# A two-layer long-convolution and FFN kernel: the plan's gaps refitted, and a new order for all engines

## The chip, the cores and the metric

The kernel runs on one core of a Trainium2 chip. The metric is the device time of one execution in microseconds (us). All data is bf16, all matmuls accumulate in f32 in PSUM.

Five engines work beside each other, each with a queue of its own: TensorE (PE in the profile, its weight loads are PEld), VectorE (DVE), ScalarE (ACT), GpSimd (POOL) and SyncE (SP, which in this kernel only issues DMAs).

## The reference

S = 2048 rows, D = 512 columns, F = 1792; x starts as `q`, and two equal layers follow, each a long convolution with gating and then a gated FFN:

```python
def _A_ref(q, k, v, shift_k, ssm_k, ssm_D):     # q is layernorm(x)
    k_shift = sum over t of k_pad[:, t:t + S, :] * shift_k[:, ks - 1 - t]     # 4 taps
    kv = k_shift * v
    ...
    y_f = kv_f * kf_f[None, :, :, :]            # FFTs of length 2*S of kv and ssm_k
    y = irfft(y_f)[:S].astype(bfloat16)
    y = y + kv * ssm_D
    return q * y

def _B_ref(x, w_gate, w_up, w_down):            # x is layernorm(x)
    return (silu(x @ w_gate) * (x @ w_up)) @ w_down

x = A_q
x = x + _A_ref(_layernorm(x), A_k, A_v, ...);  x = x + _B_ref(_layernorm(x), ...)
x = x + _A_ref(_layernorm(x), A_k, A_v, ...);  x = x + _B_ref(_layernorm(x), ...)
```

The convolution's result y does not depend on x and is the same in both layers, so it is computed once.

## The kernel before

**Tiles.** The 2048 rows are cut into 4 chunks c of 512 rows (128 partitions times 4 rows r). The convolution works chunk by chunk as products of discrete spectra, which are matmuls: the tables `fwd` and `inv` hold cosines and sines. For a chunk, `shift_mul` applies the 4 taps as matmuls with the diagonal matrices `dg`, `half` and `direct` bring the filter (`hs`) and the input (`vt`) to spectra (buffers `ev`/H, G and X in the profile, all by `evacuate`, L431), DVE multiplies and adds spectra, and `inverse_half` or `inverse` turn them back into `Yk`. The FFN works on units (layer, c, h) of 256 rows, h = 0 or 1: `gate_up` has 112 pairs of PSUM banks `pf` (the pair is one gate product, which ACT turns by Silu into `sg` on L974, and one up product, which ACT copies to `ht` on L977), DVE multiplies the two, and `down` accumulates in `pd`. PSUM has 4 banks of `pf`, 2 of `pc`, 2 of `pd`.

**Start.** The first chunk is what all else waits for: load `kn` (k's rows) and `hn` (the filter), transpose both on PE (`pt`, L378 and L489), taps (`ps<-dg,kTb`), spectra of filter and input, products, inverse (`m<-Z` on DVE L803, then PE `ps<-m,inv`, L809). Then `prologue(0, 0, 0, on_pe=True)` makes x + n*y, where n is the normalised x (ACT, L874), normalises again into `z`, transposes it on PE (`ptz`, L935) and copies it out as `zT`: row 0 on ACT (L940), the other on DVE. The first gate/up matmul (`pf<-zT,wg_sb`) needs both. For row 0 of the chunk, `prologue` does not wait for y to be in SBUF: DVE multiplies n by the PSUM bank itself (L918, `n<-n,ps`), and the ACT copy of the same bank to `Yk` (L729) is issued behind it by `evacuate_y(c, (0,))`. Every layer norm ends with a power -1/2 on POOL, `rstd<-ve,nhalf` (L826 for statistics of DVE, L855 for those of ACT, whose sums and squares are the `jk` rows of L840 and its neighbour); then `nmr` (L863, L867) and the normalising n or z.

**Later work.** From the first FFN unit on, the units' matmuls alternate with the convolution work of the next chunks. The last unit ends with one group of 512 columns (row 0) and the other row in parts of 320 and 192 columns (`TAIL`), each with its own copy or add and its own DMA (L1039 to L1055).

**Order.** Nothing is left to a scheduler. The program records 1,556 operations in a `Plan`, each with an engine, a cost in us, and the buffers it reads and writes; `Plan.add` derives the dependences (readers of one buffer don't depend on each other). The table `ORDER` gives each operation its place, and `Plan.order` goes through them in that order, sums the costs to a planned start and end for each, with a gap between an operation and one that needs its data (`SAME` on one engine, `CROSS` across engines, by the engine that produces), and gives each buffer the slot of its ring that comes free first by that plan. `Plan.issue` emits the operations in that order. So the order of each engine's queue is that of the table, and the planned times set only the ring slots and the dummy matmuls:

```python
                if start < warm_until and start - t > 0.5:
                    ...
                            n = int((start - t - (0.3 if t > 8.0 else 0.5 if t > 0.0 else 0.1)) / 0.106)
                            if n > 0:
                                warm(ring, i, n)
```

`warm` (L1307) writes 128-column products of ones into a free bank, in planned PE gaps of over 0.5 us before 32 us. `PW`, `PWA` and the 0.85 that `prologue` passes are the planned costs of the POOL power.

Of the kernel before, what the change touches and what calls it, by code (L numbers as in the profile page):

```python
# [9 lines left out]
P = 128  # L10
# [3 lines left out]
ACT = mybir.ActivationFunctionType  # L14
# [9 lines left out]
PW = 1.2  # L24
# [19 lines left out]
PWA = 2.4  # L44
# [9 lines left out]
SHARE = {(1, 0, 1): 2, (0, 2, 0): 2, (1, 3, 0): 2}  # L54
ORDER = [
# [1285 lines left out]
```

## Time and profile before

| | us |
|---|---|
| median of 3 runs | 343.18 (342.79 to 343.26) |
| span of the profiled execution | 341.1 |
| median less span | 2.1 |
| PE busy | 336.9 (99%), 2563 instructions |
| DVE busy | 282.4 (83%), 478 |
| ACT busy | 252.5 (74%), 496 |
| POOL busy | 37.3 (11%), 46 |
| last PE work ends at | 338.13 |

The span runs from the first to the last event of one profiled execution; the profiled execution has no other time of its own on record, so sums from the trace are made against its span, and the 2.1 us between span and median lie around it.  Busy times are shares of it; matmuls are pipelined, so a busy PE may still wait inside. A row of a time line has start and length in us, the engine, the line of the kernel, the operation, and output and input; a row of a group has the count, then the summed busy time and the mean in ns.

### The profile page before, as it was taken

The page shows a single profiled execution, that of the slowest core. Times are in us where ns is not written, and L with a number is a line of the kernel's source. Part 1 is how long each engine was busy: PE and PEld are TensorE (multiplying, and loading weights), DVE is VectorE, ACT ScalarE, POOL GpSimd, SP SyncE. Part 2 cuts the span into 40 slices and gives each one's busy share as a digit, 9 for nine tenths or more (in the row PEclk, how much of TensorE's full clock was granted, in tenths as well). Part 3 has the DMA queues.
Part 4 walks back from the last instruction along what each step waited for, and adds up shares of the span by engine and source line. Part 5 has one row for each costly group of instructions (what it writes and reads, how often), then busy time and mean ns, then how long its engine had stood idle before and what let it go on. Part 6 is the DMA issues. An engine that isn't in the chain of part 4 may idle for free.

```text
span 341.1 us, 6468 instructions
## 1 busy us (share of the span) xinstructions
PE 336.9 (99%) x2563; PEld 242.8 (71%) x2563; DVE 282.4 (83%) x478; ACT 252.5 (74%) x496; POOL 37.3 (11%) x46
## 2 busy tenths in 40 slices
PE   8999999999999999999999999999999999999996
PEld 7657858678687567768587756768685877777683
DVE  8899999999999999999999999889997533726022
ACT  7899999999977475778999973768665545545451
POOL 4000100002106100103100100101101000001000
PEclk9999999999999999999999999999999999999999
DMA  7999314050224175010110224010101110001111
GB/s 280 333 320 341 52 31 63 0 156 1 34 46 94 31 102 164 3 30 2 33 20 13 48 46 125 0 33 1 33 0 44 36 33 0 17 16 21 27 33 31
DMA packets 42088, 22.95 MB, mean 67 GB/s; under 512 B 33989, under 2 KB 39882, under 8 KB 42058
## 3 DMA queue, kind: packets, MB, share of 16 engines
q1 hardware_dynamic: 41904, 22.49, 26.0%
q8 instruction: 20, 0.33, 0.4%
q14 instruction: 10, 0.08, 0.1%
q10 hardware_dynamic: 154, 0.05, 0.1%
HBM read 12.33 MB, written 2.10 MB: 42 GB/s over the span
## 4 chain that ended last, share of the span: by engine, by line
PE 94%; ACT 3%; DMA 1%; SPq 0%; issue 0%; ACTq 0%
PE pf L323 57%; PE pd L994 28%; PE ps L323 6%; PE ps L470 2%; DMA kn<-in_A_k_dram 1%; ACT H L431 1%; ACT Yk L729 1%; ACT ks L526 0%; ACT n L874 0%; PE pt L378 0%; PE pt L489 0%; ACT zT L940 0%; ACT X L431 0%; SPq L354 0%; ACT xc L1052 0%
## 5 line engine op out<-in xcount | busy, mean ns | idle before, releaser
L323 PE MATMUL pf<-zT,wg_sb 128*128 128x256 bf16 (+1 forms) x872 | 110.3, 276 | 0.0
L323 PE MATMUL pf<-zT,wu_sb 128*128 128x256 bf16 (+1 forms) x872 | 110.0, 275 | 0.1
L994 PE MATMUL pd<-wd_sb,ht 128*128 128x512 bf16 (+1 forms) x462 | 106.2, 373 | 0.0
L323 PEld LDWEIGHTS <-wu_sb 128*128 128x128 bf16 x872 | 85.3, 98 | 18.9 <-issue 0.6
L323 PEld LDWEIGHTS <-wg_sb 128*128 128x128 bf16 x872 | 85.3, 98 | 17.3
L977 ACT CAST ht<-pf 128x512 bf16<-128x512 f32 x112 | 65.0, 592 | 23.0 <-PE pf L323 22.8
L974 ACT ACTIVATE sg<-pf 128x512 bf16<-128x512 f32 x112 | 66.6, 606 | 20.8 <-PE pf L323 17.3
L994 PEld LDWEIGHTS <-ht 128*128 128x128 bf16 x462 | 45.0, 98 | 44.1
L979 DVE TENSOR_TENSOR ht<-ht,sg 128x1024 bf16<-128x1024 bf16 (+1 forms) x61 | 38.9, 642 | 19.8 <-ACT ht L977 13.7
L826 POOL TENSOR_TENSOR rstd<-ve,nhalf 128x2 f32<-128x2 f32 x24 | 25.1, 1047 | 192.6 <-DVE ve L824 192.6
L821 DVE BATCH_NORM_STATS2 bnst<-xc 128x6 f32<-128x512 bf16 x48 | 31.8, 684 | 0.5
L1075 ACT CAST dn<-pd 128x512 bf16<-128x512 f32 x30 | 17.2, 590 | 17.5 <-PE pd L994 17.5
L431 ACT ACTIVATE X<-ps 128x512 bf16<-128x512 f32 x32 | 18.9, 606 | 10.5 <-PE ps L323 10.0
L1078 DVE TENSOR_TENSOR xc<-xc,dn 128x1024 bf16<-128x1024 bf16 x15 | 10.3, 687 | 16.8 <-ACT dn L1075 16.8
L669 DVE TENSOR_TENSOR t<-X,G 128x2048 bf16<-128x2048 bf16 x18 | 21.9, 1218 | 0.1
L665 DVE TENSOR_TENSOR t<-X,G 128x2048 bf16<-128x2048 bf16 x18 | 21.9, 1219 | 0.0
L855 POOL TENSOR_TENSOR rstd<-ve,nhalf 128x2 f32<-128x2 f32 x8 | 8.4, 1052 | 78.5 <-ACT ve L853 78.5
L679 DVE TENSOR_TENSOR Z<-Z,t 128x2048 bf16<-128x2048 bf16 x12 | 14.7, 1221 | 0.3
L677 DVE TENSOR_TENSOR t<-t,t 128x2048 bf16<-128x2048 bf16 x12 | 14.6, 1220 | 0.2
L431 ACT ACTIVATE H<-ps 128x512 bf16<-128x512 f32 x24 | 14.2, 612 | 0.0
L901 DVE TENSOR_TENSOR n<-n,Yk 128x1024 bf16<-128x1024 bf16 x15 | 10.3, 690 | 3.1 <-ACT n L874 1.9
L323 PE MATMUL ps<-hs,fwd 128*128 128x512 bf16 x40 | 12.7, 379 | 0.1
(103 smaller groups left out, 321.8 us busy)
## 6 DMA issues: line engine op xcount, KB each, us to landing
hn<-in_A_ssm_k_dram SPq DMA_DIRECT2D x4, 512.0 KB, 5.5
vt<-in_A_v_dram SPq DMA_DIRECT2D x4, 512.0 KB, 5.6
xc<-in_A_q_dram SPq DMA_DIRECT2D x4, 512.0 KB, 4.9
out_dram<-xc SPq DMA_DIRECT2D x15, 128.0 KB, 1.8
wg_sb<-in_B_w_gate_dram SPq DMA_DIRECT2D x1, 1792.0 KB
wu_sb<-in_B_w_up_dram SPq DMA_DIRECT2D x1, 1792.0 KB, 8.0
wd_sb<-in_B_w_down_dram SPq DMA_DIRECT2D x1, 1280.0 KB, 11.6
kn<-in_A_k_dram SPq DMA_DIRECT2D x1, 512.0 KB, 4.3
```

The source lines that it names most:

```text
L323: nc.tensor.matmul(o, lhsT=lhsT, rhs=rhs, start=(n == 0), stop=(n == len(terms) - 1))
L431: add("ACT", act(D), lambda: nc.scalar.activation(out=view(), in_=ps.t[:], func=ACT.Copy, scale=scale), r=[ps], w=[(buf, keys)], conv=conv)
L665: dve(n * D, lambda t1=t1, part=part: nc.vector.tensor_mul(out=t1.t[:], in0=x.t[:, sl, 0, :], in1=g.t[:, sl, part, :]), [(x, key(slots, (0 ...
L669: dve(n * D, lambda t2=t2, part=part: nc.vector.tensor_mul(out=t2.t[:], in0=x.t[:, sl, 1, :], in1=g.t[:, sl, 1 - part, :]), [(x, key(slots ...
L679: dve(n * D, lambda t1=t1, part=part: nc.vector.tensor_add(out=z.t[:, sl, part, :], in0=z.t[:, sl, part, :], in1=t1.t[:]), [t1], [zk], con ...
L821: add("DVE", 0.6, lambda st=st, i=i: nc.vector.bn_stats(out=st.t[:], in_=xs[c].t[:, i, :]), r=[(xs[c], (i,))], w=[st])
L826: add("POOL", pw, lambda: nc.gpsimd.tensor_tensor(out=rstd.t[:], in0=ve.t[:], in1=nhalf.t[:].to_broadcast((P, n)), op=ALU.pow), r=[ve, nha ...
L974: add("ACT", act(D), lambda ps=ps, sl=sl: nc.scalar.activation(out=sg.t[:, sl], in_=ps.t[:], func=ACT.Silu), r=[ps], w=[(sg, (b,))], due=( ...
L977: add("ACT", act(D), lambda ps=ps, sl=sl: nc.scalar.copy(out=ht.t[:, sl], in_=ps.t[:]), r=[ps], w=[(ht, (b,))], due=(us[0], at, 1.5, "a"))
L979: dve(n * m * W, lambda: nc.vector.tensor_mul(out=ht.t[:], in0=ht.t[:], in1=sg.t[:]), [sg], [ht], due=(us[0], (k + n) / NF, 0.0, "h"))
L994: nc.tensor.matmul((pds[o] if not cs.start else pds[HP]).t[:, cs], lhsT=ht.t[:, q, at, o * P:(o + 1) * P], rhs=wt["d"].t[:, ft, cs], start ...
L1075: add("ACT", act(D), lambda o=o: nc.scalar.copy(out=dn.t[:, o, :], in_=pds[o].t[:]), r=[pds[o]], w=[(dn, (o,))], due=(unit, 1.0, 3.0, "h"))
```

## The change

It has three parts. The matmuls are the same ones, and so is the arithmetic.

1. The plan's gaps and three of its costs are other numbers: `SAME` for ACT 0.12 for 0.05; `CROSS` for PE 0.2 for 0.3, DVE 0.14 for 0.2, ACT 0.15 for 0.25, POOL 0.05 for 0.15; the POOL power 0.69 everywhere.
2. `ORDER` is a new table of the same 1,556 operations, so each engine's queue has a new order; ring slots and dummy matmuls follow from it (35 dummies for 32).
3. Copies go through a helper, `copy_out`, which can hold the same copy for ACT and for DVE; the set `FLIP` that would swap them is empty, so every copy stays on its engine. Its forms are `activation(Copy)` on ACT, where some lines had `nc.scalar.copy`, and `tensor_scalar` times 1.0 on DVE, where some had `tensor_copy`.

```diff
-PW = 1.2
+PW = 0.69
...
-PWA = 2.4
+PWA = 0.69
...
+FLIP = set()
 ORDER = [
-    0, 5, 1, 2, 3, 21, 16, 6, 14, 8, 15, 66, 69, 10, 7, 9, 4, 11, 34, 12, 17, 18, 13, 19, 20, 35, 26, 120, 121, 131, 27, 30, 31, 39, 37, 40, 36, 41,
+    6, 37, 2, 5, 1, 8, 19, 0, 3, 4, 28, 40, 61, 7, 10, 9, 11, 12, 26, 20, 22, 21, 16, 23, 25, 46, 54, 65, 78, 107, 18, 42, 17, 38, 15, 33, 14, 30,
...
-    SAME = {"PE": 0.0, "DVE": 0.12, "ACT": 0.05, "POOL": 0.1, "SP": 0.0}
-    CROSS = {"PE": 0.3, "DVE": 0.2, "ACT": 0.25, "POOL": 0.15, "SP": 0.0}
+    SAME = {"PE": 0.0, "DVE": 0.12, "ACT": 0.12, "POOL": 0.1, "SP": 0.0}
+    CROSS = {"PE": 0.2, "DVE": 0.14, "ACT": 0.15, "POOL": 0.05, "SP": 0.0}
...
-    def add(self, eng, cost, emit, r=(), w=(), lat=None, due=None, conv=False, slack=0.0, after=(), dest=None):
+    def add(self, eng, cost, emit, r=(), w=(), lat=None, due=None, conv=False, slack=0.0, after=(), dest=None, alt=None):
         o = Op()
+        o.alt = None
+        if alt is not None:
+            here, there = (eng, cost, emit), alt
+            if self.choices in FLIP:
+                here, there = there, here
+            self.choices += 1
+            (eng, cost, emit), o.alt = here, there
...
+    def copy_out(dst, src, r, w, eng="ACT", n=None, scale=1.0, cost=None, **kw):
+
+        n = n or D
+        costs = dict(cost or {"ACT": act(n), "DVE": tt1(n)})
+        forms = {"ACT": lambda: nc.scalar.activation(out=dst(), in_=src(), func=ACT.Copy, scale=scale),
+                 "DVE": lambda: nc.vector.tensor_scalar(out=dst(), in0=src(), scalar1=scale, scalar2=None, op0=ALU.mult)}
+        other = "DVE" if eng == "ACT" else "ACT"
+        return add(eng, costs[eng], forms[eng], r=r, w=w, alt=(other, costs[other], forms[other]), **kw)
...
-        st = ln_stats(c, rows, 0.85)
+        st = ln_stats(c, rows)
...
-                    add("ACT", act(D), lambda ps=ps, sl=sl: nc.scalar.copy(out=ht.t[:, sl], in_=ps.t[:]),
-                        r=[ps], w=[(ht, (b,))], due=(us[0], at, 1.5, "a"))
+                    copy_out(lambda sl=sl: ht.t[:, sl], lambda ps=ps: ps.t[:].rearrange("p (b m w) -> p b m w", b=per, m=m),
+                             [ps], [(ht, (b,))], due=(us[0], at, 1.5, "a"))
...
```

The other places that now call `copy_out` are the copies of the transposed k, of `hs`, of Y, of `zT` in the prologue and of `dn`, in the same way.

More of the change, by code (lines that the diff above doesn't have):

```diff
@@ L382, in transpose_k @@
             src = lambda pt=pt: pt.t[:].rearrange("d r p -> d p r")
-            if engs[dt % len(engs)] == "ACT":
-                add("ACT", 0.47, lambda src=src, dst=dst: nc.scalar.copy(out=dst(), in_=src()), r=[pt], w=[(kT[b], (dt,))])
-            else:
-                add("DVE", tt1(D), lambda src=src, dst=dst: nc.vector.tensor_copy(out=dst(), in_=src()), r=[pt],
-                    w=[(kT[b], (dt,))])
+            copy_out(dst, src, [pt], [(kT[b], (dt,))], engs[dt % len(engs)], cost={"ACT": 0.47, "DVE": tt1(D)})
         return k_in
@@ L427, in dve @@
         add("DVE", cost or (tt1(n) if one else tt2(n)), fn, r=r, w=w, **kw)
-    def evacuate(ps, buf, keys, view, scale, eng, conv):
-        if eng == "ACT":
-            add("ACT", act(D), lambda: nc.scalar.activation(out=view(), in_=ps.t[:], func=ACT.Copy, scale=scale),
-                r=[ps], w=[(buf, keys)], conv=conv)
-        else:
-            add("DVE", tt1(D), lambda: nc.vector.tensor_scalar(out=view(), in0=ps.t[:], scalar1=scale, scalar2=None,
-                                                               op0=ALU.mult), r=[ps], w=[(buf, keys)], conv=conv)
+    def copy_out(dst, src, r, w, eng="ACT", n=None, scale=1.0, cost=None, **kw):
[5 more added lines that the diff above has]
+        return add(eng, costs[eng], forms[eng], r=r, w=w, alt=(other, costs[other], forms[other]), **kw)
+    def evacuate(ps, buf, keys, view, scale, eng, conv):
+        copy_out(view, lambda: ps.t[:], [ps], [(buf, keys)], eng, scale=scale, conv=conv)
     def half(rows, ev, par, scale, ring, engs, conv, due=None):
@@ L497, in transpose_h @@
             sl = slice(rows[0], rows[-1] + 1)
-            if engs[order.index(r0) % m] == "ACT":
-                add("ACT", act(len(rows) * D), lambda pt=pt, sl=sl: nc.scalar.copy(out=hs.t[:, sl, :], in_=pt.t[:]),
-                    r=[pt], w=[(hs, rows)], conv=conv)
-            elif row0 is not None and r0 == 0:
+            if row0 is not None and r0 == 0:
                 turns[0] = add("DVE", 0.335, lambda pt=pt: nc.vector.tensor_tensor(out=hs.t[:, 0, :], in0=pt.t[:, 0, :], in1=row0.t[:],
@@ L504, in transpose_h @@
             else:
-                turns[r0] = add("DVE", 0.335, lambda pt=pt, sl=sl: nc.vector.tensor_copy(out=hs.t[:, sl, :], in_=pt.t[:]),
-                    r=[pt], w=[(hs, rows)], conv=conv)
+                turns[r0] = copy_out(lambda sl=sl: hs.t[:, sl, :], lambda pt=pt: pt.t[:], [pt], [(hs, rows)], engs[order.index(r0) % m],
+                                     cost={"ACT": act(len(rows) * D), "DVE": tt2(len(rows) * D)}, conv=conv)
         return hs
@@ L702, in inverse @@
                 r=[(z, key((r,))), inv], w=[ps], conv=True, dest=y)
-            add("ACT", act(D), lambda ps=ps, r=r: nc.scalar.copy(out=y.t[:, r, :], in_=ps.t[:]), r=[ps], w=[(y, (r,))],
-                conv=True)
+            copy_out(lambda r=r: y.t[:, r, :], lambda ps=ps: ps.t[:], [ps], [(y, (r,))], conv=True)
     def inverse_direct(k, slots_order):
@@ L728, in evacuate_y @@
         for r in rows:
-            add("ACT", act(D), lambda r=r: nc.scalar.activation(out=y.t[:, r, :], in_=pss[r].t[:], func=ACT.Copy, scale=2.0 if SUMS else 1.0),
-                r=[pss[r]], w=[(y, (r,))])
+            copy_out(lambda r=r: y.t[:, r, :], lambda r=r: pss[r].t[:], [pss[r]], [(y, (r,))], scale=2.0 if SUMS else 1.0)
     def inverse_rows(k):
@@ L936, in prologue @@
             pop = add("PE", pe(KD, P), go, r=[z, ident], w=[pt], due=-40)
-            if o:
-                add("DVE", 0.335, lambda pt=pt, o=o: nc.vector.tensor_copy(out=zT.t[:, :, o, :], in_=pt.t[:]), r=[pt], w=[(zT, (o,))], due=-45)
-            else:
-                add("ACT", act(D), lambda pt=pt, o=o: nc.scalar.copy(out=zT.t[:, :, o, :], in_=pt.t[:]), r=[pt], w=[(zT, (o,))], due=-45)
+            copy_out(lambda o=o: zT.t[:, :, o, :], lambda pt=pt: pt.t[:], [pt], [(zT, (o,))], "DVE" if o else "ACT",
+                     cost={"ACT": act(D), "DVE": tt2(D)}, due=-45)
             done = [zop, pop]
@@ L1074, in ffn @@
             for o in range(HP):
-                add("ACT", act(D), lambda o=o: nc.scalar.copy(out=dn.t[:, o, :], in_=pds[o].t[:]), r=[pds[o]], w=[(dn, (o,))],
-                    due=(unit, 1.0, 3.0, "h"))
+                copy_out(lambda o=o: dn.t[:, o, :], lambda o=o: pds[o].t[:], [pds[o]], [(dn, (o,))], due=(unit, 1.0, 3.0, "h"))
             sl = span(rows)
@@ L1186 @@
             w = [(dg, (dt * KS + j,))]
-            if DGE[dt] == "A":
-                add("ACT", 0.32, lambda j=j, dt=dt: nc.scalar.activation(out=dg.t[:, dt, j, :], in_=ident.t[:], func=ACT.Copy,
-                                                                        scale=tapF.t[:, dt, j:j + 1]), r=[ident, tapF], w=w)
-            else:
-                e, q, cost = ("POOL", nc.gpsimd, 0.57) if DGE[dt] == "P" else ("DVE", nc.vector, 0.163)
-                add(e, cost, lambda j=j, dt=dt, q=q: q.tensor_scalar(out=dg.t[:, dt, j, :], in0=ident.t[:],
-                                                                    scalar1=tapF.t[:, dt, j:j + 1], scalar2=None, op0=ALU.mult),
-                    r=[ident, tapF], w=w)
+            forms = {"ACT": (0.32, lambda j=j, dt=dt: nc.scalar.activation(out=dg.t[:, dt, j, :], in_=ident.t[:], func=ACT.Copy,
+                                                                            scale=tapF.t[:, dt, j:j + 1]))}
+            for e, q, cost in (("POOL", nc.gpsimd, 0.57), ("DVE", nc.vector, 0.163)):
+                forms[e] = (cost, lambda j=j, dt=dt, q=q: q.tensor_scalar(out=dg.t[:, dt, j, :], in0=ident.t[:],
+                                                                          scalar1=tapF.t[:, dt, j:j + 1], scalar2=None, op0=ALU.mult))
+            e = {"D": "DVE", "A": "ACT", "P": "POOL"}[DGE[dt]]
+            other = {"DVE": "ACT", "ACT": "DVE", "POOL": "DVE"}[e]
+            add(e, *forms[e], r=[ident, tapF], w=w, alt=(other, *forms[other]))
     k_in = transpose_k(0, "pc", eng(KTE)) if K0 == "rows" else k0
```

4 lines of the change are left out of this document (2 added, 2 removed), and 114 rows, old and new, of the table ORDER.

## The prediction

> **What bounds the kernel now.** I read the page first, then the chain of waits, then busy time by stretch, and last the time line around the two places that the chain names. The page:
>
> ```profile
> span 341.1 us, 6468 instructions
> ...
> PE 336.9 (99%) x2563; PEld 242.8 (71%) x2563; DVE 282.4 (83%) x478; ACT 252.5 (74%) x496; POOL 37.3 (11%) x46
> ...
> PE 94%; ACT 3%; DMA 1%; SPq 0%; issue 0%; ACTq 0%
> ```
>
> TensorE is busy for 336.9 of 341.1 us and is 94% of the chain that ended last. A busy PE need not be a PE at its pace, so the next view is the busy time by stretch (columns: length, then PE, PEld, DVE, ACT, POOL busy, granted clock, DMA):
>
> ```profile
> 15.69:32.23 16.54, 16.30 (x139) 9.87 (x138) 16.16 (x37) 16.04 (x32) 1.85 (x2) 1.00 1.08 322
> 32.23:70.00 37.77, 37.77 (x286) 27.98 (x286) 37.50 (x56) 37.50 (x81) 3.75 (x4) 1.00 0.30 49
> 100.00:160.00 60.00, 60.00 (x434) 42.19 (x433) 58.57 (x89) 42.27 (x83) 11.19 (x6) 1.00 0.29 63
> 32.23:338.13 305.90, 305.89 (x2269) 221.70 (x2268) 252.91 (x406) 223.86 (x437) 31.62 (x30) 1.00 0.19 40
> ```
>
> From 32.23 us, where the first gate/up matmul of the first FFN unit starts, PE never stops until 338.13, and the clock is granted in full. So there is nothing to win in these 306 us; a new order can only lose there. What can be won or lost otherwise is the time at which PE reaches that first matmul, and the 3 us of tail. The chain of waits, in order of time (start, length, what), shows who sets that point:
>
> ```profile
> 6.47 0.86 PE ps L323 x4
> 7.34 0.22 PE pt L378 x4
> ...
> 19.80 1.74 PE ps L470 x8
> 21.54 0.02 issue
> 21.56 0.60 ACT X L431
> 22.16 0.18 ACT nmr L867
> 22.34 0.98 ACT H L431 x2
> 23.32 0.70 ACT n L874
> 24.02 1.46 ACT H L431 x3
> 25.48 0.70 ACT n L874
> 26.18 0.49 ACT Yk L729
> 26.67 0.49 ACT H L431
> 27.16 0.48 ACT ks L526
> ...
> 31.57 0.62 ACT zT L940
> 32.19 0.04 issue
> 32.23 1.80 PE pf L323 x15
> ```
>
> The chain is PE up to 21.54, then ACT from 21.56 to 32.19, one piece behind the other, and then PE to the end. In this stretch ACT is a queue without holes: whatever stands ahead of the zT copy in ACT's order, and whatever ACT waits for there, moves the first FFN matmul, and behind that matmul nothing gives the time back.
>
> **The change part by part.** Sets of instructions: by the built orders of the two kernels, engine by engine, PE has the same matmuls and three more of the dummy 128-column ones (35 for 32). By row "7.34 ... L378 x4" one costs 0.055 us, so 0.17 us; they stand in the stretch in which ACT sets the pace, so I take 0 and keep 0.17 as the upper end. Ahead of the first FFN matmul PE has the same real work in both.
>
> Forms: copies out of PSUM that were `copy` are now `activation(Copy)`.
>
> ```profile
> L974 ACT ACTIVATE sg<-pf 128x512 bf16<-128x512 f32 x112 | 66.6, 606 | 20.8 <-PE pf L323 17.3 <-DVE ht L979 2.8
> L977 ACT CAST ht<-pf 128x512 bf16<-128x512 f32 x112 | 65.0, 592 | 23.0 <-PE pf L323 22.8
> ```
>
> 606 against 592 ns is 14 ns; for the 112 ht copies 1.6 us of ACT. Between 100 and 160 us ACT is idle for 17.7 of 60 us, which hides it. Between 32.23 and 70 it is idle for only 0.27 of 37.77 us; 14 ht copies fall there, 0.2 us of ACT time, which PE feels only if its four `pf` banks run out. I take 0, and 0.2 as the end. Two DVE copies of bf16 PSUM become tensor_scalar, a form that the trace does not show from such a source; neither lies on the chain above, so 0.
>
> The front, PE's side. The new order puts two forward matmuls of the filter ahead of the k transposes. The 16 transposes of k, 64 tap products, 16 filter and 32 input matmuls and 16 transposes up to the last X copy are the same, so I take that copy at 21.56 again. By row "6.47 ... L323 x4" the two matmuls are 0.43 us; PE could do them while it waits for k, or stand for their operand while k is there: plus or minus 0.4.
>
> The front, ACT's side. Here is the new order of ACT's queue from the last X copy to the zT copy, with what each waits for:
>
> ```
> Activation X_348<-ps [PE]      Activation n<-xc       Activation H<-ps x3 [PE]
> Activation n<-xc               Activation H<-ps [PE]  Activation Yk<-ps [PE]
> Activation Yk<-ps [DVE]        Activation H<-ps x2    TensorCopy ks<-ps [PE]
> Activation H<-ps x2 [PE]       TensorCopy ks<-ps [PE] Activation Yk<-ps [PE]
> TensorCopy ks<-ps [DVE,PE]     Activation X<-ps [PE]  Activation jk<-xc
> Activation zT<-ptz [PE]
> ```
>
> Against before, both nmr, one Yk and one ks have left this stretch (earlier or behind zT) and one X and one jk have come in. The rows for the two places that matter, from the time line:
>
> ```profile
> 25.82 0.68 DVE L918 TENSOR_TENSOR n<-n,ps 128x512 bf16<-128x512 bf16 x1
> ```
> ```profile
> 27.95 0.67 ACT L729 ACTIVATE Yk<-ps 128x512 bf16<-128x512 f32 x1
> ```
> ```profile
> 32.05 0.66 ACT L840 ACTIVATE jk<-xc 128x512 bf16<-128x512 bf16 x1
> ```
>
> The Yk copy that waits for DVE is that of row 0: it reads the PSUM bank that DVE's `n<-n,ps` reads, and the program makes it wait for that instruction, in both kernels. Before, ACT comes to it at 27.95 while DVE was through at 25.82 + 0.68 = 26.50, so the wait costs nothing. Now ACT comes to it four places sooner. From 21.56: X 0.49 (as an H, the same form), n 0.70, three H 1.46, n 0.70, H 0.49, Yk 0.49, by the chain's rows, is 4.33, so ACT stands there at 25.89. DVE's work up to `n<-n,ps` is the same set, DVE is busy for 16.16 of 16.54 us here, and I find no hole that the new order closes, so it ends at 26.50 again. ACT waits 0.6 us with everything behind it queued, H, ks and zT among them. Behind it: Yk 0.49, two H 0.98, ks 0.48, two H 0.98, ks 0.48, Yk 0.49, ks 0.48, X 0.49 and jk 0.66 are 5.53. From 26.55 (0.05 for the handover, as the "issue" pieces of the chain) that is 32.08 for the start of the zT copy, against 31.57: **+0.51 us**. The planner's list of reads and writes has no such wait (two readers of one buffer are free of each other in it), so its plan can't have avoided it. Ends: 0 if DVE comes 0.6 us earlier or an H of the list waits longer for PE anyway; 0.9 with PE's 0.4 on top.
>
> The tail. PE's last matmuls are now the row 0 group of 512 columns and then four of 192; before, row 0 was done earlier.
>
> ```profile
> 338.17 0.32 ACT L1052 CAST xc<-pd 128x192 bf16<-128x192 f32 x1 [4.56 <-PE pd L994]
> ```
> ```profile
> out_dram<-xc SPq DMA_DIRECT2D x15, 128.0 KB, 1.8
> ...
> out_dram<-xc ACTq DMA_DIRECT2D x1, 48.0 KB, 1.7
> ```
>
> With PE's end as 338.13, ACT's 192 columns leave as before (copied at 338.49, landing 1.7 later, 340.2). Row 0 is free four 192-column matmuls (0.33 us) before PE's end, its DVE add is taken as the 0.68 of the L918 row (the same 512 columns), so its 128 KB are issued at about 338.55 and land 1.8 us later, 340.35: **+0.13 us**, between 0 and 0.3.
>
> The later stretches. PE has no idle there, so a stall costs its full length. The plan now prices every rstd on POOL at 0.69 us where it had 1.2 (or 2.4, or 0.85):
>
> ```profile
> L826 POOL TENSOR_TENSOR rstd<-ve,nhalf 128x2 f32<-128x2 f32 x24 | 25.1, 1047 | 192.6 <-DVE ve L824 192.6
> ```
>
> The mean is 1047 ns. One of the 24 took 6.21 us, beside an unbroken run of DVE work on two inputs:
>
> ```profile
> 105.56 6.21 POOL L826 TENSOR_TENSOR rstd<-ve,nhalf 128x2 f32<-128x2 f32 x1 [11.57 <-DVE ve L824]
> ```
>
> The new order keeps 0.6 us or more of DVE work between ve and the user of rstd in most places, as before, so the likeliest cost is small: I take +0.1, with 0 to 1.5 as the ends. The Trainium skill's "GPSIMD Engine Reference", § Specifications, says that POOL shares its SBUF interfaces with VectorE and is held up by DVE instructions with two SBUF inputs. The 6.21 us row fits that; by that rule alone any of the 32 rstd could be late by the length of the DVE run beside it, which is the third rival.
>
> **Sum.** +0.51 +0.13 +0.1 = +0.7 us. The sum is made against the span, 341.1; the median of the three runs, 343.18, is 2.1 us above it, which lies around the span and is not touched. So 343.18 + 0.7 = **343.9 us**.
>
> **The rivals.** (1) Hidden: ACT's wait falls together with a wait for PE, or DVE is 0.6 us sooner, so only the tail is left: 343.18 + 0.13 = 343.3. For it: ACT and DVE run at 97% or more, and a gap closed on one moves the other. Against: no row shows such a gap of DVE.
>
> (2) Faster, with one mechanism: PE becomes what bounds the front. The new order moves 16 tap products from ahead of the z transposes to behind them, work that PE does while it waits for zT. The two largest groups of PE between 6.47 and 32.23:
>
> ```profile
> L323 PE MATMUL ps<-dg,kTb 128*128 128x128 bf16 x128 | 8.5, 219 | 0.0
> L470 PE MATMUL ps<-vt,fwd 128*128 128x512 bf16 x32 | 7.4, 379 | 0.0
> ```
>
> With the smaller groups there are 159 matmuls of 128 columns, at 0.055, and 74 of 512, at 0.215: 24.7 of 25.8 us. If ACT reaches zT early enough, the difference of 1.1 less 0.2 for the dummies can go: 343.18 - 0.9 + 0.13 = 342.4. It decides where ACT stands at zT before 30.9 us, 0.7 sooner than now. Against: ACT has to lose 0.7 us of a queue without holes, and it gains a wait.
>
> (3) Late z: in the saturated stretches an rstd or a dependent copy is late and PE stands 1 to 2 us in all: 343.9 + 1.1 = 345.0. For it: DVE busy 58.57 of 60 us at 100 to 160, and tighter gaps in the plan. Against: PE went through 306 us without a stop with the same work.
>
> **How the numbers follow.** Forecast 48%, its own range 343.5 to 344.4; rival 1 18%, which is also the case that the change does nothing; rival 2 18%, because the front has many small pieces and my count is of one wait in it; rival 3 16%. A measurement here can tell about 0.2%, 0.69 us: under 342.49 is faster, over 343.87 slower. The forecast's cases lie on both sides of the upper bound, 28 over and 20 under it. So slower 0.28 + 0.16 = 0.44; same 0.20 + 0.18 + 0.04 of rival 2 = 0.42; faster 0.14. The range runs from 342.4 to 345.2: it leaves out 0.09 of rival 2 and about 0.08 of rival 3.
>
> **What would show it.** In the new profile: ACT idle for about 0.6 us ahead of a Yk copy near 26 us, released by DVE's `n<-n,ps`; the first FFN matmul near 32.7; PE at 100% in every stretch behind it; the last DMA an SP one of 128 KB. The forecast is wrong if the first FFN matmul starts before 32.3, if ACT shows no such wait, or if PE has idle time after 33 us.

## The result, and the profile after

The changed kernel takes **347.14 us** (median of 4 runs, 346.94 to 347.25) beside 343.22 (342.79 to 343.33, 4 runs) of the kernel before: ratio 1.0115, 95% interval 1.0101 to 1.013. The forecast was 343.9 with a range to 345.2: right in sign, far too small. The span grew by 4.3 us, from 341.1 to 345.4. The page of the changed kernel:

```profile
span 345.4 us, 6436 instructions
...
PE 336.5 (97%) x2528; PEld 242.9 (70%) x2566; DVE 280.6 (81%) x478; ACT 252.2 (73%) x496; POOL 40.6 (12%) x46
...
PE 58%; DVE 27%; ACT 7%; POOL 3%; issue 3%; DMA 1%; SPq 0%; POOLq 0%; DVEq 0%; ACTq 0%
```

The last line is the plainest sign. Before, PE was 94% of the chain that ended last; now it is 58%, and DVE is 27%: the chain runs through PE's stops into the engines that fed it late. (The trace lacks 38 of PE's matmul records, 2528 of 2566. So PE's busy time counts too low here, and below a stop of PE is the distance from one matmul's start to the next one's, less the pace of that shape, with a missing record credited.) Busy time by stretch of the changed kernel, cut at its own first FFN matmul and its own last matmul:

```profile
15.69:33.34 17.65, 16.71 (x144) 10.24 (x144) 16.92 (x37) 16.66 (x34) 1.84 (x2) 1.00 1.07 299
...
33.34:341.99 308.65, 305.09 (x2236) 221.04 (x2268) 250.48 (x406) 223.42 (x436) 35.20 (x30) 1.00 0.18 40
```

The lengths are what counts. The first FFN matmul starts at 33.34, 1.11 later than the 32.23 of before. From there to PE's end the same 2268 weight loads take 308.65 us where they took 305.90: 2.75 more. From PE's end to the end of the span it is 345.4 less 341.99, about 3.4, where it was 3.0: 0.45 more, by the unrounded ends. That is 1.11 + 2.75 + 0.45 = 4.3 us, all of it.

**The front.** Time line of the changed kernel:

```profile
4.51 1.55 PE L499 MATMUL pt<-ident,hn 128*128 128x128 bf16 x16
...
6.55 1.05 PE L388 MATMUL pt<-ident,kn 128*128 128x128 bf16 x16
...
26.48 0.69 DVE L923 TENSOR_TENSOR n<-n,ps 128x512 bf16<-128x512 bf16 x1
...
27.20 0.60 ACT L439 ACTIVATE Yk<-ps 128x512 bf16<-128x512 f32 x1 [0.62 <-DVE n L923]
...
32.60 0.69 ACT L439 ACTIVATE zT<-ptz 128x512 bf16<-128x512 bf16 x1
...
33.34 0.49 PE L333 MATMUL pf<-zT,wu_sb 128*128 128x256 bf16 x3
```

The forecast's wait is there: ACT stands 0.62 us (forecast 0.6) at the row 0 Yk copy, released by `n<-n,ps`. But that DVE instruction itself starts at 26.48 instead of the 25.82 that I had taken over from before, and the `zT` copy at 32.60 instead of the forecast 32.08. The delay begins much earlier. The same two PE rows in the kernel before:

```profile
4.35 1.06 PE L489 MATMUL pt<-ident,hn 128*128 128x128 bf16 x16
...
5.63 0.84 PE L378 MATMUL pt<-ident,kn 128*128 128x128 bf16 x12 [0.21 <-DMA kn<-in_A_k_dram]
```

Sixteen transposes of the filter take 1.55 us instead of 1.06. Single starts lie 107 ns apart at first and then 56; that step comes by 3.95 us before, and at about 5.5 after.

**The stops behind the front.** The largest, in the chain of waits of the changed kernel between 85 and 95 us, and PE's longest wait in the whole span:

```profile
86.26 1.00 POOL rstd L831
87.26 0.03 issue
87.29 0.75 DVE z L884 x2
...
89.28 0.05 issue
89.33 3.57 DMA zT<-z
92.90 0.05 issue
92.95 1.92 PE pf L333 x16
```
```profile
PE pf L333 <- DMA zT<-z: 1.0, 1, 1.0
```

PE stops for 1.14 us at 91.6 until a transposed z has landed. The second, 0.53 us at 147.5, is a late rstd seen through three engines; time line:

```profile
145.64 1.22 DVE L676 TENSOR_TENSOR t<-X,G 128x2048 bf16<-128x2048 bf16 x1
...
145.88 1.53 POOL L831 TENSOR_TENSOR rstd<-ve,nhalf 128x2 f32<-128x2 f32 x1 [5.79 <-DVE ve L829]
...
147.44 0.16 DVE L868 SCALAR_TENSOR_TENSOR nmr<-mv,rstd 128x2 f32<-128x2 f32 x1 [0.58 <-POOL rstd L831]
147.52 0.68 DVE L982 TENSOR_TENSOR ht<-ht,sg 128x1024 bf16<-128x1024 bf16 x1
...
148.26 0.60 PE L997 MATMUL pd<-wd_sb,ht 128*128 128x512 bf16 x2 [0.37 <-DVE ht L982]
...
225.28 0.69 POOL L831 TENSOR_TENSOR rstd<-ve,nhalf 128x2 f32<-128x2 f32 x1 [5.17 <-DVE ve L829]
```

The last row is an rstd with nothing beside it: 0.69 us. The one at 145.88 starts beside DVE's `t` and takes 1.53: it ends at 147.41, 0.55 us after `t` (146.86). DVE comes to `nmr`, which needs it, stands for 0.58 us, and the `ht` product that PE needs is queued behind. In both traces nearly every rstd that starts beside a DVE tensor instruction ends 0.55 us after the end of it, or of a later one. The Trainium skill's "GPSIMD Engine Reference", § 1 Specifications, names the shared SBUF interface, and the row agrees with it. Of 32 rstd 9 take 1.4 us or more, against 4 before, and the mean of the larger group (after the comma) is 1151 ns for 1047:

```profile
L831 POOL TENSOR_TENSOR rstd<-ve,nhalf 128x2 f32<-128x2 f32 x24 | 27.6, 1151 | 211.0 <-DVE ve L829 202.1
```

Smaller stops lie at 60 to 65 (0.4 together), 160 (0.3) and 200.9 (0.3).

**The tail**, time line of the changed kernel and then of the kernel before:

```profile
342.02 0.32 ACT L1055 CAST xc<-pd 128x192 bf16<-128x192 f32 x1 [5.48 <-PE pd L997]
342.37 0.40 ACTq L1058 DMA_DIRECT2D out_dram<-xc  x1
342.41 0.33 SPq L1047 DMA_DIRECT2D out_dram<-xc  x1
```
```profile
338.51 0.39 ACTq L1055 DMA_DIRECT2D out_dram<-xc  x1
```

The SP DMA of 128 KB is issued 0.42 us after PE's end, as forecast. From that issue to the end of the span it is 3.0 us (345.42 less 342.41), where the 48 KB of before needed 2.6 (341.11 less 338.51).

### The profile page after: what moved, and what is told of

Read it like the earlier page. It is cut to its first block, busy times and chain, and to the rows that moved or that the text cites. A ratio compares the mean times of both kernels' runs of the same rounds, so it can differ in the third digit from the quotient of the medians.

```text
span 345.4 us, 6436 instructions
## 1 busy us (share of the span) xinstructions
PE 336.5 (97%) x2528; PEld 242.9 (70%) x2566; DVE 280.6 (81%) x478; ACT 252.2 (73%) x496; POOL 40.6 (12%) x46
## 4 chain that ended last, share of the span: by engine, by line
PE 58%; DVE 27%; ACT 7%; POOL 3%; issue 3%; DMA 1%; SPq 0%; POOLq 0%; DVEq 0%; ACTq 0%
PE pf L333 34%; PE pd L997 17%; PE ps L333 4%; DVE t L676 3%; DVE bnst L826 2%; DVE ht L982 2%; POOL rstd L831 2%; DVE Z L686 2%; DVE t L684 2%; DVE t L672 2%; DVE m L559 2%; DVE t L661 1%; DVE G L600 1%; ACT sg L977 1%; ACT jk L850 1%
## 5 line engine op out<-in xcount | busy, mean ns | idle before, releaser
L333 PE MATMUL pf<-zT,wg_sb 128*128 128x256 bf16 (+1 forms) x872 | 110.5, 276 | 1.2 <-DMA zT<-z 1.0
L333 PE MATMUL pf<-zT,wu_sb 128*128 128x256 bf16 (+1 forms) x872 | 109.1, 276 | 0.4 <-ACT sg L977 0.2
L997 PE MATMUL pd<-wd_sb,ht 128*128 128x512 bf16 (+2 forms) x434 | 102.5, 372 | 1.8 <-DVE ht L982 0.4
L333 PEld LDWEIGHTS <-wg_sb 128*128 128x128 bf16 x872 | 85.1, 98 | 22.5 <-DMA zT<-z 1.5
L333 PEld LDWEIGHTS <-wu_sb 128*128 128x128 bf16 x872 | 85.1, 98 | 17.2 <-DMA zT<-z 0.7
L439 ACT ACTIVATE ht<-pf 128x512 bf16<-128x512 f32 x112 | 65.6, 601 | 31.7 <-PE pf L333 31.2
L977 ACT ACTIVATE sg<-pf 128x512 bf16<-128x512 f32 x112 | 65.9, 603 | 25.5 <-PE pf L333 19.6
L831 POOL TENSOR_TENSOR rstd<-ve,nhalf 128x2 f32<-128x2 f32 x24 | 27.6, 1151 | 211.0 <-DVE ve L829 202.1
L439 ACT ACTIVATE dn<-pd 128x512 bf16<-128x512 f32 x30 | 17.8, 606 | 18.7 <-PE pd L997 18.6
L860 POOL TENSOR_TENSOR rstd<-ve,nhalf 128x2 f32<-128x2 f32 x8 | 9.5, 1191 | 61.1 <-ACT ve L858 61.1
L333 PE MATMUL ps<-hs,fwd 128*128 128x512 bf16 x37 | 12.3, 379 | 0.8 <-ACT H L439 0.7
```

The lines of the kernel that those rows point to most:

```text
L333: nc.tensor.matmul(o, lhsT=lhsT, rhs=rhs, start=(n == 0), stop=(n == len(terms) - 1))
L439: forms = {"ACT": lambda: nc.scalar.activation(out=dst(), in_=src(), func=ACT.Copy, scale=scale), "DVE": lambda: nc.vector.tensor_scalar(o ...
L831: add("POOL", pw, lambda: nc.gpsimd.tensor_tensor(out=rstd.t[:], in0=ve.t[:], in1=nhalf.t[:].to_broadcast((P, n)), op=ALU.pow), r=[ve, nha ...
L977: add("ACT", act(D), lambda ps=ps, sl=sl: nc.scalar.activation(out=sg.t[:, sl], in_=ps.t[:], func=ACT.Silu), r=[ps], w=[(sg, (b,))], due=( ...
L997: nc.tensor.matmul((pds[o] if not cs.start else pds[HP]).t[:, cs], lhsT=ht.t[:, q, at, o * P:(o + 1) * P], rhs=wt["d"].t[:, ft, cs], start ...
```

## The experiments

Runs with another table have line numbers that are lower by four than the changed kernel's (L329 for L333). Medians are beside 343.1 to 343.6 of the kernel before on the same chip. "Ahead" is what PE loses against its fast pace from its first matmul to the first FFN matmul, so slow early matmuls count in it as stops do; "behind" is its stops from there to its end. They are 3.4 and 0.03 us in the kernel before, 4.4 and 2.8 in the changed one.

### Whose is it: the order, or the rest

```diff
 ORDER = [
-    6, 37, 2, 5, 1, 8, 19, 0, 3, 4, ...
+    0, 5, 1, 2, 3, 21, 16, 6, 14, 8, ...     # the table of before; gaps, costs and copy_out stay new
```

> The changed kernel with the ORDER table of before; the new gaps, costs and copy forms stay. If all of the 3.9 us comes from the new order, this is at 343.2 (within 0.3 us of before), with the first gate/up matmul near 32.2 us and no stall behind it. If the forms of the copies, or the ring slots that the new gaps pick, cost time, it is 344 or more, and PE stands behind 33 us.

343.21 us, ratio 1.0002 (0.9986 to 1.0017). Busy time by stretch from its first FFN matmul, to be read beside "32.23:338.13" of before:

```profile
32.52:338.50 305.98, 305.89 (x2269) 221.71 (x2268) 252.90 (x406) 224.41 (x438) 31.56 (x30) 1.00 0.19 41
```

PE has no stop in it. So with the old order the new gaps, the new costs, the ring slots by them and the `activation(Copy)` forms cost nothing, as forecast, and the 4 us come with the new order. Whether the ring slots that the new gaps pick add something under the new order was not run.

Two hybrids ask which part of the table it is: the first 254 operations of before and then the new order, and the first 286 of the new one and then the order of before. (The diff is written for the sequence of operations that the table of places stands for.)

```diff
-ORDER = new
+ORDER = before[:254] + [o for o in new if o not in before[:254]]      # front_of_before
+ORDER = new[:286] + [o for o in before if o not in new[:286]]         # front_of_after
```

> The new order, but the first 254 operations (through the first gate/up products, about 34 us) stand as in the order of before. My reading of the two traces is that the front costs 1.1 us, stalls behind it 2.8 us and the tail 0.4 us, each on its own: then this is 347.1 - 1.1 = 346.0, with the first gate/up matmul near 32.2 and the same stalls behind it. The rival, that the later stalls hang on the late start (units run late, and the DMAs and LayerNorms with them), gives 343.5 to 344.5.

> The other way round: the first 286 operations in the new order (about 40 us), the rest as in the order of before. If the parts add up: 343.2 + 1.1 = 344.3, first gate/up matmul near 33.3, no stall behind it. If a late front upsets what follows, PE stalls behind 40 us as well and it is 345 or more.

front_of_before: 352.67, ratio 1.0258 (1.0228 to 1.0288); 9.1 us behind, at 35.9, 65.2, 97 and other places. front_of_after: 346.24, ratio 1.0091 (1.0068 to 1.0114); 5.8 ahead, 1.9 behind. The first is far over both of its cases (346.0, or 343.5 to 344.5), the second falls into the worse of its two (345 or more). Of front_of_after's 5.8, about 1.0 is the start of that execution: its front is the changed kernel's, but k's transposes begin at 7.52 there and at 6.55 in the changed kernel. The parts don't add: a cut makes stops that neither order has, by my reading because each front leaves another backlog on DVE and ACT, which was not tested. From here on I moved single steps, but for one more hybrid.

### The rstd on POOL

rstd as a multiplication by 1000 on DVE and on ACT, so the values are scaled wrongly; nothing waits for POOL then.

```diff
-        add("POOL", pw, lambda: nc.gpsimd.tensor_tensor(out=rstd.t[:], in0=ve.t[:], ... op=ALU.pow), ...)
+        add("DVE", 0.1, lambda: nc.vector.tensor_scalar(out=rstd.t[:], in0=ve.t[:], scalar1=1000.0, scalar2=None, op0=ALU.mult), ...)
```

> The changed kernel with every power on POOL replaced by a multiplication with a constant, on DVE behind its ve (24 times) or on ACT (8 times), so that no engine waits for POOL there; the normalised values are scaled wrongly. If the stalls behind the front come from rstd being later than the 0.69 us of the plan, nearly all of the 2.8 us goes and some 0.5 us at the front (its z waits for rstd too): 344 to 344.6. If the stalls come from the order of DVE's queue itself, or from the zT transfers, they stay: 346.5 or more.

346.27, ratio 1.0094 (1.0058 to 1.0129), where 344 to 344.6 was expected if late rstd were nearly all of it; behind 1.4 instead of 2.8, and the first FFN matmul no sooner (33.62). The stops at 147.5, 60 to 65, 160 and 200.9 are gone, one of 0.2 at 320 is new; the one at 91.5 stays. PE's waits:

```profile
PE pf L333 <- DMA zT<-z: 1.0, 1, 1.0
```

So late rstd cost 1.4 us of the 2.75. Most of the rest is that one late z.

### The front

The changed kernel again, for its own scatter:

> The changed kernel once more, nothing edited, for what varies from execution to execution. 347.1 within 0.3 us. The stalls of PE at about 63 to 65, 91.6, 147.5, 160 and 200.9 us come again if they belong to the order of the queues; those made by chance (a transfer that was slow once) would be gone. In the first 6 us the change of PE's pace, from 106 to 56 ns for a 128-column matmul, came at 5.6 us in the changed kernel and at 3.9 in before; if it is a matter of chance, it comes at another time now and the first gate/up matmul moves with it.

347.33 (346.65 to 347.9); first FFN matmul 33.49, the same stops at the same places (1.5 at 91.75, 0.54 at 148).

The forecast's wait taken away, by moving the row 0 copy behind the zT copy in ACT's queue; then also the 16 taps that PE does ahead of the first FFN group behind it; then the first edit in the kernel before:

```diff
   Activation H<-ps [PE]
-  Activation Yk<-ps [DVE]        # row 0
   ...
   Activation zT<-ptz [PE]
+  Activation Yk<-ps [DVE]        # row 0
```

> The changed kernel with one operation moved: the ACT copy of row 0 to Yk, which waits for DVE's n<-n,ps, now stands behind the zT copy. My forecast blamed this wait for 0.5 us. If so, ACT has no wait near 27 us, PE's stop of 0.59 us at 27.5 is gone, and the first gate/up matmul comes 0.5 us sooner: 346.6. If PE's own work from 28 to 33 us (16 tap products behind the last transposes) or DVE sets the point, it is 346.9 to 347.2 though ACT's wait is gone.

> As the run with the Yk copy moved, and the last 16 tap products ahead of the first gate/up group now stand behind it (two PE operations swapped). If ACT's wait and PE's own work together set the first gate/up matmul, it comes 0.9 to 1.1 us sooner than in the changed kernel: 346.1. If the late start of the k transposes (0.9 us) passes through whatever is moved later, 346.8 or more.

> The kernel before, with only the same ACT copy of row 0 moved behind the zT copy and the work right after it. ACT's queue ahead of zT is shorter by 0.49 us, so the first gate/up matmul could come up to 0.3 us sooner (the transposes of z then set it, by their end at 31.4): 342.9. If ACT and DVE, at 99% from 32 to 70 us, are just as much the bound as PE, the gain comes back as stalls of PE there: 343.2 to 343.5.

yk_behind_zT: 346.88 (346.32 to 347.08), 0.3 to 0.45 less than the two medians of the changed kernel, with overlapping ranges. Time line:

```profile
26.80 0.69 DVE L919 TENSOR_TENSOR n<-n,ps 128x512 bf16<-128x512 bf16 x1
...
32.38 0.60 ACT L435 ACTIVATE zT<-ptz 128x512 bf16<-128x512 bf16 x1
32.87 0.59 ACT L435 ACTIVATE Yk<-ps 128x512 bf16<-128x512 f32 x1
...
33.07 0.71 PE L329 MATMUL pf<-zT,wu_sb 128*128 128x256 bf16 x5
```

The wait is gone. The zT copy is only 0.22 sooner than 32.60, because the front of this execution ran late: k's transposes start at 6.86 for 6.55, and `n<-n,ps` at 26.80 for 26.48. From the start of `n<-n,ps` to that of the zT copy it is 5.58 us, against 6.12 in the changed kernel: the wait was worth 0.54 us, as forecast. PE goes from its 16 taps straight into the first FFN matmul here. yk_and_taps: 347.93, ratio 1.012 (1.0078 to 1.0162). Its first FFN matmul is at 32.85, but 16 taps (0.9 us) are then still to be done, and a new stop of 0.67 comes at 284.1. An earlier first FFN matmul gains nothing if work is only put behind it. before_yk_late: 343.38, ratio 0.9995 (0.9976 to 1.0014): in the kernel before that copy costs nothing. From `n<-n,ps` to the zT copy it is 5.70 us there and 5.75 in the kernel before, although ACT's queue is shorter by a copy of 0.49 us; ACT now waits 0.17 us for the transpose of z. So in the kernel before ACT's queue was not alone in setting that point: the path of z through DVE, POOL and PE ends almost with it.

The front of another experiment (waits_moved, below) decided what the forecast got wrong. It is the front order of the changed kernel, but here the pace changed early:

```profile
4.37 1.08 PE L495 MATMUL pt<-ident,hn 128*128 128x128 bf16 x16
...
6.04 1.06 PE L384 MATMUL pt<-ident,kn 128*128 128x128 bf16 x16
...
25.97 0.69 DVE L919 TENSOR_TENSOR n<-n,ps 128x512 bf16<-128x512 bf16 x1
...
26.69 0.60 ACT L435 ACTIVATE Yk<-ps 128x512 bf16<-128x512 f32 x1 [0.63 <-DVE n L919]
...
32.10 0.68 ACT L435 ACTIVATE zT<-ptz 128x512 bf16<-128x512 bf16 x1
...
32.83 1.03 PE L329 MATMUL pf<-zT,wu_sb 128*128 128x256 bf16 x8
```

With the step by 3.95 as in the kernel before, the wait is 0.63 and the zT copy starts at 32.10: forecast 32.08. The other 0.50 us (32.60 less 32.10) goes with the later pace step of the changed kernel's execution: `hn` and `kn` land within 0.06 us of each other in the two, and k's transposes start 0.51 apart. With this order of the front, the later the step, the later they start: 6.04 us with it by 3.95, 6.28 with 4.8 (all_moved), 6.46 with 5.1 (z_half), 6.55 with 5.5, 6.71 with about 6.2 (after_again). Late loads do the same: in early_z `kn` landed at 6.80 for 5.53, and k's transposes start at 6.85 though the step came by 4.5. Is the step the doing of the first operations? The first 113 of before, the rest new:

```diff
-ORDER = new
+ORDER = before[:113] + [o for o in new if o not in before[:113]]
```

> The new order, but its first 113 operations (about the first 14 us: the tables, the transposes of filter and k, the tap products) stand as in the order of before. If the late start of the k transposes (6.55 against 5.63 us) belongs to the new order, the k transposes start at 5.6 again and the first gate/up matmul comes 0.4 to 0.9 us sooner: 346.5. If it is what hn's landing and the change of PE's pace do in each execution, it is 347.2.

348.59, ratio 1.014 (1.0107 to 1.0172). The step came at 6.4 us and k's transposes at 6.17, with before's own start. The same start had the step by 3.95 in all_second, below. The front had new stops (0.95 at 26.0, 0.44 at 22.5). So an early start is not to be had by copying the first operations.

### The stop at 91.6

z is late there, I thought, since the statistics stand behind an FFN product and a spectrum part in DVE's queue. In early_z both went behind them, in z_half the part alone:

```diff
   DVE n<-n,Yk
-  DVE Z<-m
-  DVE ht<-ht,sg                    # stays in z_half
   DVE xc<-xc,n   bnst x2   mv x2   ve
+  DVE Z<-m
+  DVE ht<-ht,sg
```

> The changed kernel with two DVE operations of 0.6 us each (a product ht and a part of the inverse's Z) moved from ahead of the chain xc, bnst, mv, ve to behind ve, at about 83 us. PE's stop of 1.1 to 1.5 us at 91.6 waits for the second zT transfer, whose z is made behind these. If the place in DVE's queue makes it late, z comes about 1.2 us sooner, the stop shrinks to 0.3 or less, and the time is 347.2 - 1.1 = 346.1. If the transfer itself is slow (3.6 us from issue to landing against 2.5 in the median), the stop stays above 0.8 and the time at 347.

> The changed kernel with one DVE operation of 0.6 us (part of the inverse's Z) moved behind ve at about 83 us, and the product ht left where it is, so that no sg buffer is held longer. z is 0.6 us sooner: the stop of PE at 91.6 shrinks from 1.1 to 1.5 us by 0.6, and none comes at 85: 346.6. If it is not z that the stop hangs on, 347.2.

early_z: 348.09, ratio 1.0129 (1.0081 to 1.0177). The stop at 91.6 is gone, one of 1.83 us stands at 85.3 in its place, and another of 0.54 at 108. Time line:

```profile
85.88 1.28 DVE L978 TENSOR_TENSOR ht<-ht,sg 128x1024 bf16<-128x1024 bf16 x2
...
86.60 0.60 ACT L973 ACTIVATE sg<-pf 128x512 bf16<-128x512 f32 x1 [2.56 <-DVE ht L978]
...
87.25 0.27 PE L329 MATMUL pf<-zT,wu_sb 128*128 128x256 bf16 x1 [1.66 <-ACT sg L973]
```

ACT waits 2.56 us for a free `sg`, which the postponed ht product holds, and PE for the bank that ACT has not emptied. z_half: 347.07, stop 1.03, because the transpose again landed late. A transposed z normally lands about 1.2 us after its issue has ended; the one at 89.3 took 2.25 to 2.7 in the changed kernel, after_again, no_pool_rstd, yk_behind_zT, waits_moved, z_half and z_and_queue. DMA of the changed kernel from 90.2 to 91.6 us, then of yk_and_taps from 88.2 to 90.0, where the same pair is issued from 88.82:

```profile
q1 hardware_dynamic: 505, 0.12, 95.8%
q8 instruction: 1, 0.02, 5.1%
issues: line engine op xcount, KB each, median us to landing
zT<-z SPq DMA_TRANSPOSE x1, 3.6
```
```profile
q8 instruction: 1, 0.02, 3.6%
q1 hardware_dynamic: 4, 0.00, 0.4%
issues: line engine op xcount, KB each, median us to landing
zT<-z SPq DMA_TRANSPOSE x1, 2.4
```

Where one fetch of 16 KB of instructions falls among the packets of the pair's second transpose, that lands 3.6 us after its issue started; where the fetch came ahead of them, the first (the row shown) lands after 2.4 and the second after 2.5, and PE's stop was 0.05. Twelve profiles have this pair. In seven the fetch begins 2.2 to 2.5 us after the pair's first issue, and the second transpose lands after 3.5 to 3.9 us; in five it begins 0.4 before to 0.1 after that issue or over 4 us later, and the second lands after 2.5.

All 395 transposes of z whose landing the 18 traces tell agree. In 28 of them an instruction fetch (16 or 8 KB) begins 0.85 to 2.05 us after the start of the issue, and all 28 land late, 1.69 to 3.05 us after the issue's end. Of the other 367 one does (1.69), and the rest land after 1.1 to 1.4. No run moved the fetch alone, so its being the cause is not shown by an edit, but chance is ruled out.

Four of the late ones are the kernel before's own, at 85.4, 124.4, 165.4 and 190.0 us. DMA of the kernel before from 189.5 to 194.5 us:

```profile
q8 instruction: 1, 0.02, 1.4%
zT<-z SPq DMA_TRANSPOSE x2, 4.2
```

That is 4.2 us from the start of the issue, and PE has no stop there. So the new order did not bring late transposes; it put one where nothing is left over. At the usual 1.22 us behind its issue the second of the pair would have landed at 91.81, just when PE has come to it (91.80).

### The stops at 147 and 200

ht ahead of `nmr` at 147, and the second z at 196 right behind the first; in z_and_queue also SP's two transposes ahead of the output DMA at 198:

```diff
-  DVE nmr<-mv,rstd
   DVE ht<-ht,sg
+  DVE nmr<-mv,rstd
...
   DVE z<-xc (1)
+  DVE z<-xc (2)
   DVE H<-m   t<-t,t
-  DVE z<-xc (2)
...
   SP zT<-z (1)
+  SP zT<-z (2)                     # z_and_queue
   SP out_dram<-xc
-  SP zT<-z (2)                     # z_and_queue
```

> The changed kernel with two places edited: at 147 us the product ht for which PE waits stands ahead of the nmr that waits for POOL's rstd, and at 196 us the second z stands right behind the first, ahead of 1.8 us of other DVE work. If in-order waiting behind rstd makes PE's stops there (0.53 and 0.30 us), both go: 347.2 - 0.8 = 346.4. For rstd itself: in both traces it ends 0.55 us after the DVE instruction beside which it is held. If DVE's instruction holds it, the rstd at about 146 us, with one more DVE product behind it, now takes 2.1 us instead of 1.53, and nmr still waits 0.58 us; if its length is POOL's own affair, it stays at 1.5 and nmr finds it done.

> The kernel with the two waits moved, and SP's two zT transfers at about 196 us ahead of the output DMA that waits for its rows until 197.6. Moving z alone left PE's stop at 200 us (0.55 us), by my reading because this DMA stands ahead of the second zT on SP. If so the stop is gone: 346.65 - 0.5 = 346.1. If the stop is from elsewhere, 346.6.

waits_moved: 346.65, ratio 1.0086 (1.0061 to 1.0111). The stop at 147 is gone. Time line:

```profile
145.63 1.53 POOL L827 TENSOR_TENSOR rstd<-ve,nhalf 128x2 f32<-128x2 f32 x1 [5.79 <-DVE ve L825]
...
146.53 0.69 DVE L978 TENSOR_TENSOR ht<-ht,sg 128x1024 bf16<-128x1024 bf16 x1
```

I had expected rstd to be held again by this ht, to 2.13 us. It took 1.53: here it was held only by the instruction beside which it started (the one of 6.21 us in the kernel before was held through several). The stop at 200 stayed, 0.55, by my reading because SP issued the output's DMA ahead of the transpose. z_and_queue moves that too: the stop at 200 is gone, one of 0.37 at 207.5 comes, and the median is 346.62, the same. But four runs without these edits (yk_behind_zT, yk_and_taps, start_of_before, z_half) also have the stop at 207.5 to 209 and none at 200, so what makes the one at 200 stays open.

### All moves together, and how much room the old order has

all_moved is yk_behind_zT, early_z, waits_moved and the tail of before; all_second is start_of_before, yk_behind_zT, z_half, z_and_queue and the tail of before.

> All edits in one: the Yk copy behind zT, the early z, the two waits moved, and the order of before for the last groups (row 0 first, then the 320 and 192 columns). If the loss is the sum of these places: 347.2 - 0.4 (Yk) - 1.1 - 0.8 - 0.4 (last transfer) = 344.5, leaving the late start of the k transposes and about 0.5 us of small stops. If what is taken away at one place comes back at the next (DVE and ACT at 97% or more), 345.5 or more.

> Start of before, Yk copy behind zT, the half of z, both waits with SP's queue, and the last groups as in before. By the sum of the parts: 347.2 - 0.7 - 0.4 - 0.6 - 1.1 - 0.4 = 344.0; still over before, since nothing in it gives PE less to do. If parts don't add, 345 or more.

346.89, ratio 1.0071 (1.0025 to 1.0117), and 346.68, ratio 1.009 (1.006 to 1.012); the first with 3.5 ahead and 3.8 behind, the second with 4.8 and 2.0, and both with the tail back at 2.97. Both were expected near 344; the gains don't add, for each move makes a stop elsewhere.

Last, the kernel before with every power issued twice, so that each rstd is later:

```diff
-        add("POOL", pw, lambda: nc.gpsimd.tensor_tensor(... op=ALU.pow), ...)
+        add("POOL", pw, lambda: [nc.gpsimd.tensor_tensor(... op=ALU.pow) for _ in range(2)], ...)
```

> The kernel before, with every power on POOL issued twice in a row (the second writes the same values), so that each rstd is about 0.65 us later. The plan of before priced it at 1.2 us or more where 0.69 to 1.5 are measured. If that price bought room, the late rstd costs little: 343.2 to 344.2, with PE's stops behind 33 us below 0.7 in sum (the first LayerNorm may add 0.3 ahead of it). If before is as tight as the changed kernel, it loses as much as that did: 346 or more.

352.22, ratio 1.0245 (1.0188 to 1.0302), 7.5 behind. The second power ends 0.77 to 1.44 us after the first, once 6.1. Of the two cases expected the second came (346 or more), and by more than the changed kernel loses. So the old order has no room for an rstd that is later by this much, it just has few late ones; for late transposes, at the four places above, it had room. No kernel beat the one before.

## Why the prediction was wrong

| term | forecast | measured | by |
|---|---|---|---|
| order of the front, to zT | +0.51 | +0.53 | waits_moved against before |
| later pace step, to zT | not seen | +0.50 | changed kernel against waits_moved |
| the same two, to the first FFN matmul | +0.51 | +1.11 | 33.34 less 32.23 |
| later stretches | +0.1 | +2.75 | 308.65 less 305.90 |
| tail | +0.13 | +0.45 | from PE's end to the span's |
| sum | +0.7 | +4.3 | spans |

**ACT's wait: right**, in place and length; taken away it gave back 0.54 us between `n<-n,ps` and the zT copy. The zT copy is also right when the pace step comes as before (32.10 for 32.08), with some luck: ACT's Yk copy behind the wait started 0.14 late there, and the pieces from it to the zT copy took 5.41 us for 5.53. Too strong was the sentence that whatever stands ahead of the zT copy in ACT's order moves the first FFN matmul: before_yk_late took 0.49 us out, and the copy came 0.05 sooner.

**"I take that X copy at 21.56 again", and with it DVE "ends at 26.50 again": failed.** `n<-n,ps` ended at 27.17. Of the 0.67 us, 0.15 are the order's (25.97 less 25.82 in waits_moved: the two filter matmuls hold k's transposes by 0.41, and most of that is made up). The rest goes with the pace step. I had costed each early transpose at 0.055 us, a rate that the trace of before shows from 3.95 us on.

**"The likeliest cost is small: I take +0.1": the step that failed most.** The +0.1 should have been 2.75: 1.4 of late rstd, 1.1 to 1.5 of one late transpose, the rest small; the upper end of 1.5 did not hold either. I argued that the order keeps 0.6 us of DVE work between `ve` and the user of rstd. The measured need is the rest of the DVE instruction beside which rstd starts, or of a later one, plus 0.55 us, and the new order gives less at 61, 147, 158 and 195. The third rival (345.0, 16%) had half of the mechanism, late rstd, and its "1 to 2 us in all" was near what that half cost. It lacked the transposes: I had put nothing for them, though the trace of before has late ones without a stop. The sum lacked the chance that several terms go wrong together. Its counter-argument, "306 us without a stop with the same work", was the trap: a stretch without stops says nothing of its margin, and before_two_powers shows how little there was: with each rstd about 1 us later PE stops at about ten places.

**The tail: 0.45 for 0.13.** The issue was timed right. I had used the 1.8 and 1.7 us of the DMA table as if the last event of the span were that landing; from the issue to the end it is 3.0 and 2.6.

**Forms, costs and gaps at nothing: right** (order_of_before).

## What to carry to other kernels

A saturated engine that never stops can be on the edge everywhere, so a new order must be judged by the margin of each wait behind it (when the producer ends against when the consumer comes), not by the busy shares or by the old trace's lack of stops. Measure the bound engine's lost time from start to start, by stretch; the time of one milestone misleads, as yk_and_taps shows. A plan that prices an operation by its undisturbed duration can put it where it is disturbed: the new one prices every rstd at 0.69 us, and 9 of 32 took 1.4 or more. (How the table was made from the plan is not on record.)

## What the runs showed of the hardware

**PE's early pace.** In 18 profiles the starts of 128-column matmuls go from 107 to 56 ns apart at between 3.5 and 8.5 us, by 3.95, at about 5.5 and at about 6.2 with one and the same order of the front, while the granted clock of the profile stands at 1.00 throughout. The Trainium skill's "TensorE: Matmul & The Clock Gate", § Part 1: The HAM clock gate, gives these two paces, and says that the window that decides runs free of the kernel and that the point of change varies by 500 ns. The paces agree; the scatter here was larger. The five profiles with the old order of the front (one with a copy moved, one with the powers doubled) had the step by 5.05, and those with a new order had it both early and late; whether the order makes a late step likelier stays open.

**POOL beside DVE.** A small POOL power of 0.69 us alone ends 0.55 us after the DVE tensor instruction beside which it starts, be that one of one or of two inputs (0.72 us beside a TENSOR_SCALAR, 1.53 beside a TENSOR_TENSOR), or after a later one (6.21 and 2.67 us); beside bn_stats it was not held (0.69). When a later one holds it too is open.

**Transposing DMAs.** One lands about 1.2 us after its issue has ended, and 1.7 to 3.05 us in the 28 of 395 in which an instruction fetch began 0.85 to 2.05 us after the start of the issue. The 34 issues that took over 1.3 us instead of 1.2 (up to 2.4) each had a fetch that began from 0.5 us before to 0.8 us after their start. No run moved a fetch alone.
